# Inverting the sums of exponentials six queries a partition, by way of DRAM, in a routed attention with a squared-ReLU network

## Chip, cores and metric

One core of a Trainium2 chip runs the kernel. The metric is the device time of one execution in microseconds. Before the change the median of three runs is 980.3 us (980.09 to 983.05); the profiled execution spans 978.4 us.

## What is computed

The reference is attention in which a query sees only the keys that have the same nearest centroid, followed by a network with a squared ReLU. There are 4 batches, 8 heads, 768 positions, 64 columns a head and 16 centroids a head.

```python
q_assign = np.argmax(np.einsum('bhsd,hcd->bhsc', q_n, c_n), axis=-1)
k_assign = np.argmax(np.einsum('bhsd,hcd->bhsc', k_n, c_n), axis=-1)
mask = q_assign[:, :, :, None] == k_assign[:, :, None, :]
scores = np.where(mask, scale * q @ k.T, -1e9)
attn = np.exp(scores - np.max(scores, axis=-1, keepdims=True))
attn = attn / (np.sum(attn, axis=-1, keepdims=True) + 1e-09)
x = (attn @ v) laid out as (batch * position, head * column)   # 3072 x 512
h = np.maximum(x @ w_in, 0.0)                                  # 512 -> 2048
out = (h * h) @ w_out                                          # 2048 -> 512
```

The division by the sum is the step that the change is about. The kernel does it after the product with v: it multiplies that product by the inverse of the sum.

## The kernel before

Two heads are worked together as a pair, so there are 16 pairs, four to a batch. A pair's 768 queries are split into two halves of 384 (`h`), and its 768 keys into six chunks of 128, taken two at a time (`c` = 0, 2, 4). One (pair, h, c) is a unit; a pair of the later batches has six units in a row. The list `units` (L711) holds them, and the main loop (L779) walks over it. In each turn it emits, in this order: the scores of unit u, the scaling of halves that were finished earlier (`ends`, L770), the products with v of units that are one or two turns behind, the sums of halves whose v products are complete (`add_up`, L523), rounding of weights, and pieces of other work: the preparation of the next pair (`prep`) and, from L842 and L846, the network of batch 0, which fills TensorE between the attention's products. The networks of batches 1 to 3 follow after the attention (L883), and have their own products (L662, L693).

The order in which instructions stand on each engine is then set by a scheduler that goes by this order of emission, by priorities, and by the buffers that are free. Each engine runs its instructions strictly in the order that results, and nearly all DMA is issued by SyncE's one queue, in order too: a transfer that waits for its data holds up all those behind it.

What the steps around the change do, for pairs 4 to 15 (batches 1 to 3):

- `scores` (L439): TensorE writes the scores of a unit, two key chunks by two heads, into two PSUM tiles `sc` (L447, run by `together`, whose lines are L91 and L94). ScalarE takes the exponential in place (L466). VectorE multiplies by the mask and moves the result to SBUF, one instruction a chunk and head, four a unit (`ex`, L470). The mask compares `qid`, the centroid number of every query, spread over all partitions, with `ids`, those of the keys. There are only two `sc` tiles, so the scores of the next unit wait until `ex` has read this unit's. GpSimd adds up `ex` into `acc` (L480, L482).
- `times_v` (L497): products of `ex` with v, into a PSUM tile `av` for each half. The pool of `av` holds two.
- `add_up` (L523): four products with a column of 2^40 sum `acc` over its partitions, into a PSUM tile `sm` (L532). `sm` has four groups of 32 partitions, one for each head and half of the 384 queries, and each row of a group holds the same 192 sums. VectorE inverts all 128 x 192 of them (`r`, L537). One row of each group goes to DRAM (`far_r`, L540), and comes back spread over 64 partitions a head (`rb`, L543), so that it can multiply `av`, which has columns of v on partitions and queries along the free axis. A copy of the four rows goes to `seen` (L544), for a check at the end that all sums are in range.
- `finish` (L553): VectorE multiplies `av` by `rb` and writes the result to `xT` (L556), which is the network's input. It is emitted one turn after `add_up`, by way of the list `added` (L793, L815).
- The preparation of a pair: q and k are loaded (L109), rewritten by ScalarE (`flat`, L277) and sent to DRAM (`words`, L278), and come back through a DMA that transposes (`qkT`, L288). Products with the centroids (`lg`), a copy (`lgs`, L307), transposes (`lt`) and four VectorE instructions (`mx`, `best` twice, `ids`, L340 to L347) number the clusters; `ids_b` (L359), one transpose, `row` (L401), `far` (L403) and `qid` (L404) spread the numbers of the queries.

Two halves end in each cycle of six units: the second half of a pair (its `sm` comes when the next pair is in its third unit) and the first half of the next (two units later).

Of the kernel before, what the change touches and what calls it, by code (L numbers as in the profile page):

```python
# [8 lines left out]
F32 = mybir.dt.float32  # L9
# [9 lines left out]
P = 128  # L19
# [6 lines left out]
def kernel(  # L26
# [10 lines left out]
    nc = tc.nc  # L37

    B, H, S, D = q.shape
# [6 lines left out]
    HP = H // 2  # L46
    NB = NCH // 2
    TB = NB * P
    NG = B * HP
# [13 lines left out]
    small = ctx.enter_context(tc.tile_pool(name="small", bufs=2))  # L63
# [5 lines left out]
    rbp = ctx.enter_context(tc.tile_pool(name="rbp", bufs=2))  # L69
# [6 lines left out]
    dram = ctx.enter_context(tc.tile_pool(name="dram", bufs=2, space=bass.MemoryType.DRAM))  # L76
# [4 lines left out]
    def bank(name, shape):  # L81
        return ps_f.tile(shape, F32, name=name, tag="f")
# [5 lines left out]
    def together(products, offset=2000):  # L88

        products = iter(products)  # L90
        last = nc.tensor.matmul(**next(products))  # L91
        with tc.high_priority(offset=offset):
            for product in products:
                last = nc.tensor.matmul(**product)  # L94
        return last.ins
# [82 lines left out]
    for _ in range(8):  # L178
# [14 lines left out]
        out=odd[:, 1:2], in0=row_i, scalar1=1.0 / C, scalar2=None, op0=ALU.mult  # L193
    )
    constants = nc.vector.tensor_scalar(
        out=odd[:, 0:1], in0=odd[:, 1:2], scalar1=-1.0, scalar2=1.0, op0=ALU.mult, op1=ALU.add
    ).ins

    seen = const.tile([8 * NG, TB // 2], F32, name="seen")
# [233 lines left out]
    def first_half(pair, h):  # L433
        return pair < HP and h == 0
# [51 lines left out]
    def ones_products(sm, e, rhs, first, last):  # L486

        n, rows = TB // 2, P // 4
        return [
            dict(  # L490
                out=sm[rows * (2 * e + g) : rows * (2 * e + g + 1)], lhsT=ups[:, 0:rows],
                rhs=rhs[:, n * g : n * (g + 1)], start=first, stop=last,
            )
            for g in range(2)
        ]
# [25 lines left out]
    spread_out = {}  # L521

    def add_up(pair, h):  # L523


        b, hp = divmod(pair, HP)
        if first_half(pair, h):
            sm = sums.pop((pair, h))
            nc.scalar.copy(out=xT_of(b, h)[:, hp], in_=av.pop((pair, h)))
        else:  # L530
            total = acc.pop((pair, h))
            sm = bank("sm", [P, TB // 2])  # L532
            one = [ones_products(sm, e, total[:, e], True, True) for e in range(2)]
            together([p for both in zip(*one) for p in both])
        row = 4 * (2 * pair + h)
        r = once.tile([P, TB // 2], F32, name="r")
        nc.vector.reciprocal(out=r, in_=sm)  # L537
        r = r.rearrange("(r p) n -> r p n", r=4)[:, 0]
        far = dram.tile([2, TB], F32, name="far_r")
        nc.sync.dma_start(far.rearrange("e (g n) -> (e g) n", g=2), r)  # L540
        rb = rbp.tile([P, TB], F32, name="rb")
        for e in range(2):
            nc.sync.dma_start(rb[D * e : D * (e + 1)], far[e].partition_broadcast(D))  # L543
        nc.sync.dma_start(seen[row : row + 4], r)  # L544
        spread_out[pair, h] = rb

    def xT_of(b, h):
        if (b, h) not in xT:
            pool = {0: xtp, 1: xt_first, 2 * B - 1: xtp}.get(2 * b + h) or later["xT"]
            xT[b, h] = pool.tile([P, KT, TB], F32, name="xT")  # L550
        return xT[b, h]

    def finish(pair, h):  # L553
        b, hp = divmod(pair, HP)
        x = xT_of(b, h)[:, hp]
        nc.vector.scalar_tensor_tensor(  # L556
            out=x, in0=av.pop((pair, h), x), scalar=UP, in1=spread_out.pop((pair, h)),
            op0=ALU.mult, op1=ALU.mult,
        )
# [5 lines left out]
    def ffn(b, h):  # L565
        gT = []
        for f in range(FT):
            ph = bank("ph", [P, TB])
            for kk in range(KT):
                nc.tensor.matmul(  # L570
                    ph, lhsT=w_in[:, kk, f * P : (f + 1) * P], rhs=xT[b, h][:, kk],
                    start=(kk == 0), stop=(kk == KT - 1),
                )
                if kk < KT - 1:
                    yield TB
            gT.append(gtp.tile([P, TB], F32, name="gT"))
            nc.scalar.activation(out=gT[f], in_=ph, func=ACT.Relu)
            nc.scalar.square(gT[f], gT[f])
            yield TB
        for i in range(NB):  # L580
            po = bank("po", [P, DM])
            for f in range(FT):
                nc.tensor.matmul(  # L583
                    po, lhsT=gT[f][:, i * P : (i + 1) * P], rhs=w_out[:, f],
                    start=(f == 0), stop=(f == FT - 1),
                )
                if f < FT - 1:
                    yield DM
            osb = later["out"].tile([P, DM], F32, name="osb")
            nc.scalar.copy(out=osb, in_=po)  # L590
            nc.sync.dma_start(out_view[b, h * NB + i], osb)
            yield DM
# [148 lines left out]
    def behind_first(u, what=last_logits):  # L741
        return tc.issue_after(what[0]) if u == 0 else ExitStack()
# [23 lines left out]
    added = []  # L766
# [3 lines left out]
    def ends(halves):  # L770
        for pair, h in halves:
            b, hp = divmod(pair, HP)

            with tc.high_priority(offset=1000) if (pair, h) == (HP - 1, 0) else ExitStack():
                finish(pair, h)
            if hp == HP - 1 and (b, h) in PLAIN:
                fill.append(ffn(b, h))

    for u in range(len(units) + 3):  # L779
        if u < len(units):  # L780
            pair, h, c = units[u]
            if (p := next_pair(u)) is not None:
                ahead.extend(prep(p))
            if u in (TWOS, TWOS + 2):

                split_words(HP, int(u > TWOS))
            if c == 0 and u + 3 < len(units) and units[u + 3][0] not in raw_v:
                load_v(units[u + 3][0])

            with behind_first(u):  # L790
                scores(pair, h, c)

        ends(added)  # L793
        added.clear()
        if u < TWOS:
            ready = u - 1
        elif u == TWOS or u % 2 or u >= len(units):
            ready = u

        complete, late = late, []  # L800
        while v_next < min(ready, len(units)):
            pair, h, c = units[v_next]
            times_v(pair, h, c)
            v_next += 1
            if c == NCH - 2:
                (late if h and not HP * NCH <= u < len(units) else complete).append((pair, h))
        for pair, h in complete:
            with tc.high_priority(offset=1000) if first_half(pair, h) else ExitStack():
                add_up(pair, h)
            if h == 1:  # L810
                for d in (qkT, ids, qid):
                    d.pop(pair)
            if h == 1 or pair < HP:
                raw_v.pop(pair)
            added.append((pair, h))  # L815

        rounding += 4
        while rounding >= 3:
            rounding -= 3
            i = next(to_round, None)  # L820
            if i is not None:
                with tc.issue_after(last_exp[0]):
                    round_weights(i)
                if (i := next(loaded, None)) is not None:
                    load_weights(i)
            elif not later:
                early.close()
                for name, bufs in (("xT", 5), ("out", 2)):
                    later[name] = keep.enter_context(
                        tc.tile_pool(name=name + "_late", bufs=bufs, side="right",  # L830
                                     reuse_waits="tile")
                    )
        share = 0
        if u % 2 == 0 or not TWOS < u < len(units):
            n = 2 if TWOS < u < len(units) else 1
            share = max(0, left[0] - RESERVE) * sum(map(density, range(u, u + n)))
            share //= max(1, sum(map(density, range(u, ENDS))))
        goal = left[0] - share

        for i in range(3):  # L840
            if i == 2:
                fill_steps(share * 2 // 3)  # L842
            if ahead:
                with behind_first(u, masked if i else last_logits):
                    (ahead.pop(0) or int)()
        fill_steps(left[0] - goal)  # L846
# [235 lines left out]
```

## Time and profile before

| | us | |
|---|---|---|
| span | 978.4 | |
| TensorE busy | 958.9 | 98% |
| VectorE busy | 562.2 | 57% |
| GpSimd busy | 375.9 | 38% |
| ScalarE busy | 315.4 | 32% |
| r, L537 | 43.4 | 32 x 1357 ns |
| xT, L556, idle before it, waiting for rb | 50.3 | 26 times |

The span has two parts. Up to 538 us attention and the network of batch 0 share the engines; from 538 us to the end the products of L662 and L693 run without a gap, and the chain of work that ended last is these products alone, 44% of the span. In the first part that chain goes through TensorE's products too, and for 13 us before 533 us through r, far_r, rb, xT, ex and acc of the last pair.

In the lists of groups and waits a time is a sum over all instructions of the group, and idle time is given with what ended it. A wait is named after the instruction that waits and the one it waited for. In the timeline the columns are start, duration, engine, line, operation, names, shapes, count, and in brackets the idle time before the first with its releaser; several instructions in a row are merged, and then the duration is that of them all. SPq is the queue of SyncE: there the duration is that of issuing the transfer, and not of the transfer.

### The profile page before, as it was taken

The numbers are of one execution on the slowest core, as the hardware profiler recorded it, in microseconds if no ns is written. First come the engines' busy times: TensorE is split into PE (matmuls) and PEld (weight loads), VectorE is DVE, ScalarE is ACT, GpSimd is POOL, SyncE is SP. The second block draws the span as 40 slices with busy tenths as digits, with TensorE's granted clock in tenths as the row PEclk, the third lists the DMA queues.
The fourth block names the chain that finished last, engine by engine and source line by source line (L and its number), as shares of the span: only waits on it lengthen the run. The fifth ranks groups of instructions, "written<-read, shape, count | busy, mean of one in ns | idle before, by whom it ended". The sixth has DMA issues, their size and how long they took to land.

```text
span 978.4 us, 12070 instructions
## 1 busy us (share of the span) xinstructions
PE 958.9 (98%) x4479; PEld 552.0 (56%) x4479; DVE 562.2 (57%) x913; ACT 315.4 (32%) x511; POOL 375.9 (38%) x277
## 2 busy tenths in 40 slices
PE   7998999999999999999999999999999999999997
PEld 4544444434444444443344556888556888556886
DVE  5767867666566665658654866531556531656331
ACT  5886756344345555544231211000111000111000
POOL 1337757555656556555557331002231002231000
PEclk9999999999999999999999999999999999999999
DMA  9757782444545444443210000000000000000000
GB/s 242 214 180 217 184 200 63 114 116 122 133 115 131 110 119 122 121 115 88 61 37 18 18 1 0 13 26 27 0 1 1 22 22 21 1 1 0 22 22 25
DMA packets 127746, 74.54 MB, mean 76 GB/s; under 512 B 90944, under 2 KB 119104, under 8 KB 127680
## 3 DMA queue, kind: packets, MB, share of 16 engines
q1 hardware_dynamic: 125968, 73.26, 28.3%
q8 instruction: 38, 0.62, 0.3%
q10 hardware_dynamic: 1712, 0.43, 0.2%
q14 instruction: 28, 0.23, 0.1%
HBM read 48.27 MB, written 15.86 MB: 66 GB/s over the span
## 4 chain that ended last, share of the span: by engine, by line
PE 50%; DVE 0%; DMA 0%; POOL 0%; issue 0%; SPq 0%; DVEq 0%; POOLq 0%
PE bank L693 22%; PE bank L662 22%; PE po L583 3%; PE sc L91 1%; PE sc L94 1%; PE av L91 1%; PE av L94 1%; POOL acc L482 0%; DMA rb<-far_r 0%; DVE ex L470 0%; PE sm L91 0%; DMA far_r<-r 0%; DVE r L537 0%; PE lg L91 0%; SPq L543 0%
## 5 line engine op out<-in xcount | busy, mean ns | idle before, releaser
L482 POOL TENSOR_TENSOR acc<-acc,ex 128x768 f32<-128x768 f32 x112 | 205.4, 1834 | 111.0 <-DVE ex L470 97.8
L470 DVE SCALAR_TENSOR_TENSOR ex<-qid,ids,sc 128x384 f32<-128x384 bf16 x288 | 158.0, 609 | 66.6 <-ACT sc L466 48.6
L466 ACT ACTIVATE sc<-sc 128x768 f32<-128x768 f32 x144 | 108.3, 793 | 162.3 <-PE sc L94 144.6
L94 PE MATMUL sc<-qkT 64*128 64x384 f32 x576 | 152.8, 506 | 0.5
L94 PE MATMUL av<-ex,v_raw 128*64 128x384 f32 x576 | 135.6, 491 | 0.0
L651 POOL TENSOR_TENSOR w_s<-w_in 128x256 f32<-128x256 f32 x24 | 18.4, 765 | 276.4 <-PE bank L693 162.0
L632 DVE TENSOR_TENSOR g<-bank,g 128x384 f32<-128x384 f32 x144 | 77.8, 555 | 80.7 <-PE bank L662 79.7
L570 PE MATMUL ph<-xT,w_in 128*128 128x384 f32 x256 | 93.2, 506 | 3.5 <-DVE xT L556 2.8
L693 PE MATMUL bank<-w_out,g 128*128 128x256 f32 x432 | 95.2, 379 | 0.0
L583 PE MATMUL po<-w_out,gT 128*128 128x512 f32 x192 | 92.3, 612 | 0.0
L91 PE MATMUL sc<-qkT 64*128 64x384 f32 x192 | 87.5, 536 | 3.8 <-DVE ex L470 3.8
L693 PEld LDWEIGHTS bank<-w_out,g 128*128 128x128 f32 x432 | 82.1, 190 | 11.8
L632 DVE TENSOR_TENSOR osb<-bank,osb 128x256 f32<-128x256 f32 x54 | 22.1, 423 | 107.6 <-PE bank L693 102.2
L94 PEld LDWEIGHTS sc<-qkT 64*128 64x128 f32 x576 | 65.4, 187 | 27.3 <-issue 4.8
L91 PE MATMUL av<-ex,v_raw 128*64 128x384 f32 x192 | 80.4, 500 | 0.0
L570 PEld LDWEIGHTS ph<-xT,w_in 128*128 128x128 f32 x256 | 46.5, 192 | 43.3 <-issue 13.3
L662 PE MATMUL bank<-xT,w_in 128*128 128x384 f32 x192 | 69.8, 487 | 0.0
L662 PE MATMUL bank<-x_t,w_s 128*128 128x384 f32 x192 | 69.7, 486 | 0.0
L662 PE MATMUL bank<-xT,w_s 128*128 128x384 f32 x192 | 69.7, 486 | 0.0
L480 POOL TENSOR_TENSOR acc<-ex 128x768 f32<-128x768 f32 x28 | 50.8, 1814 | 49.0 <-DVE ex L470 39.8
L94 PEld LDWEIGHTS av<-ex,v_raw 128*64 128x64 f32 x576 | 49.3, 137 | 34.5 <-issue 34.4
L693 PE MATMUL bank<-w_t,g 128*128 128x256 f32 x288 | 65.1, 379 | 0.0
(127 smaller groups left out, 1218.5 us busy)
## 6 DMA issues: line engine op xcount, KB each, us to landing
words<-flat SPq DMA_DIRECT2D x24, 384.0 KB
w_raw<-in_moe_w_in_dram SPq DMA_DIRECT2D x16, 512.0 KB
w_raw<-in_moe_w_out_dram SPq DMA_DIRECT2D x16, 512.0 KB
v_raw<-in_v_dram SPq DMA_DIRECT2D x20, 384.0 KB
rb<-far_r SPq DMA_DIRECT2D x64, 96.0 KB
q_raw<-in_q_dram SPq DMA_DIRECT2D x31, 192.0 KB
k_raw<-in_k_dram SPq DMA_DIRECT2D x31, 192.0 KB
out_dram<-osb SPq DMA_DIRECT2D x23, 256.0 KB
```

Source lines behind the costliest of these rows:

```text
L91: last = nc.tensor.matmul(**next(products))
L94: last = nc.tensor.matmul(**product)
L466: last_exp[0] = nc.scalar.activation(out=t[:, 2 * i : 2 * i + 2] if pair < HP else src, in_=src, func=ACT.Exp, scale=SCALE).ins
L470: nc.vector.scalar_tensor_tensor(out=t[:, 2 * i + e], in0=qid[pair][1][:, h, e], scalar=ids[pair][:, ch % NB, 2 + ch // NB, e : e + 1], in ...
L480: nc.gpsimd.tensor_tensor(out=acc[pair, h], in0=t[:, 0:2], in1=t[:, 2:4], op=ALU.add)
L482: nc.gpsimd.tensor_tensor(out=acc[pair, h], in0=acc[pair, h], in1=t[:, 2 * i : 2 * i + 2], op=ALU.add)
L570: nc.tensor.matmul(ph, lhsT=w_in[:, kk, f * P : (f + 1) * P], rhs=xT[b, h][:, kk], start=(kk == 0), stop=(kk == KT - 1),)
L583: nc.tensor.matmul(po, lhsT=gT[f][:, i * P : (i + 1) * P], rhs=w_out[:, f], start=(f == 0), stop=(f == FT - 1),)
L632: nc.vector.tensor_tensor(out=out, in0=bank, in1=to, op=ALU.add)
L651: nc.gpsimd.tensor_tensor(out=s1, in0=a[1][0], in1=a[1][1], op=ALU.add)
L662: nc.tensor.matmul(bank, lhsT=operands[j][0][:, kk], rhs=operands[j][1][:, kk], start=(kk == 0), stop=(kk == H2 - 1),)
L693: nc.tensor.matmul(bank, lhsT=operands[j][0][:, f], rhs=operands[j][1][:, f], start=(f == 0), stop=(f == F2 - 1),)
```

## The change

In pairs 4 to 14 (`HP <= pair < NG - 1`) the sums are no longer inverted where they are. ScalarE copies the 128 x 192 tile from PSUM (`r`), one row of each group goes to DRAM as sums (`far_s`), and comes back laid out with 64 partitions a head and six queries on each (`few`, 128 x 6). VectorE inverts these six columns. They go to DRAM again (`far_r`), and from there `rb` and `seen` are read as before. The reciprocal thus works on 6 elements a partition instead of 192, and the path from `sm` to `rb` has two round trips through DRAM instead of one. To give it time, the scaling of these halves is emitted two turns behind instead of one. Pairs 0 to 3 and pair 15 keep the old way.

```diff
         row = 4 * (2 * pair + h)
         r = once.tile([P, TB // 2], F32, name="r")
+        if HP <= pair < NG - 1:
+
+            nc.scalar.copy(out=r, in_=sm)
+            far_s = dram.tile([2, TB], F32, name="far_s")
+            nc.sync.dma_start(
+                far_s.rearrange("e (g n) -> (e g) n", g=2),
+                r.rearrange("(r p) n -> r p n", r=4)[:, 0],
+            )
+            few = small.tile([P, 2 * TB // P], F32, name="few")
+            nc.sync.dma_start(few, far_s.rearrange("e (p j) -> (e p) j", p=P // 2))
+            nc.vector.reciprocal(out=few, in_=few)
+            far = dram.tile([2, TB], F32, name="far_r")
+            nc.sync.dma_start(far.rearrange("e (p j) -> (e p) j", p=P // 2), few)
+            rb = rbp.tile([P, TB], F32, name="rb")
+            for e in range(2):
+                nc.sync.dma_start(rb[D * e : D * (e + 1)], far[e].partition_broadcast(D))
+            nc.sync.dma_start(seen[row : row + 4], far.rearrange("e (g n) -> (e g) n", g=2))
+            spread_out[pair, h] = rb
+            return
         nc.vector.reciprocal(out=r, in_=sm)
...
-        ends(added)
-        added.clear()
+        ends([e for due, e in added if due <= u])
+        added[:] = [(due, e) for due, e in added if due > u]
...
-            added.append((pair, h))
+            added.append((u + (2 if HP <= pair < NG - 1 else 1), (pair, h)))
```

## The prediction

> **What bounds the kernel now.** I read the page's busy times first, then the waits of TensorE and VectorE in the stretch that the change touches, then the timeline around single waits. From the page and from the waits of TensorE alone between 200 and 540 us:
>
> ```profile
> PE 958.9 (98%) x4479; PEld 552.0 (56%) x4479; DVE 562.2 (57%) x913; ACT 315.4 (32%) x511; POOL 375.9 (38%) x277
> ```
>
> ```profile
> PE sc L91 <- DVE ex L470: 3.5, 3, 2.5
> PE sm L91 <- POOL acc L482: 0.4, 1, 0.4
> ```
>
> TensorE sets the end: in 340 us it waits 3.9 us. VectorE waits much more in the same stretch (waits of VectorE, 200 to 540 us), but hides it:
>
> ```profile
> DVE xT L556 <- DMA rb<-far_r: 35.8, 20, 3.3
> DVE ex L470 <- DMA qid<-far: 8.7, 2, 4.5
> ```
>
> So removing VectorE work or waits pays only where TensorE waits for VectorE. It does so three times, always a score product (L91) waiting for ex (L470), which must leave the two score banks first: 0.55 us at 225.89, 0.43 at 407.90, 2.48 at 466.27. The timeline of TensorE at the last, and the stretches (us, busy of PE, PEld, DVE, ACT, POOL, clock, DMA) around it:
>
> ```profile
> 466.27 0.61 PE L91 MATMUL sc<-qkT 64*128 64x384 f32 x1 [2.48 <-DVE ex L470]
> ```
>
> ```profile
> 463.23:466.64 3.41, 0.93 (x6) 0.33 (x4) 3.41 (x5) 0.00 (x0) 1.02 (x1) 1.00 1.20 223
> 466.64:470.05 3.41, 3.41 (x10) 1.17 (x7) 1.84 (x5) 1.59 (x2) 2.66 (x2) 0.50 0.13 27
> ```
>
> After the idle window one window runs at clock 0.50 and loses half of 3.41, 1.7 us more. The first two waits follow qid, which the queue issued behind the transpose (waits of VectorE of 4.13 and 4.54 us for it). All that can be won is about 0.8 + 0.6 + 2.5 + 1.7 = 5.6 us.
>
> How tight ex is elsewhere shows in an ordinary pair, timeline of VectorE:
>
> ```profile
> 231.12 1.36 DVE L537 RECIPROCAL r<-sm 128x192 f32<-128x192 f32 x1 [1.14 <-PE sm L94]
> 232.89 2.19 DVE L470 SCALAR_TENSOR_TENSOR ex<-qid,ids,sc 128x384 f32<-128x384 bf16 x4 [0.41 <-ACT sc L466]
> 236.52 0.56 DVE L340 TENSOR_REDUCE mx<-lt 128x24 f32<-128x384 f32 x1 [1.44 <-PE lt L317]
> 237.80 0.56 DVE L556 SCALAR_TENSOR_TENSOR xT<-av,rb 128x384 f32<-128x384 f32 x1 [0.72 <-DMA rb<-far_r]
> ...
> 240.13 2.19 DVE L470 SCALAR_TENSOR_TENSOR ex<-qid,ids,sc 128x384 f32<-128x384 bf16 x4
> ```
>
> Its queue:
>
> ```profile
> 230.23 0.39 SPq L278 DMA_DIRECT2D words<-flat  x1
> 232.50 0.55 SPq L540 DMA_DIRECT2D far_r<-r  x1
> ...
> 234.16 1.12 SPq L543 DMA_DIRECT2D rb<-far_r  x2
> ```
>
> The ex of 240.13 ends at 242.32; TensorE's next scores take the second bank at 242.38. The slack is nil, although TensorE shows no wait.
>
> [...]far_r usually takes 1.6 to 1.65 us to land, 1.96 where it was issued at 353.75 and words had landed only at 355.16.[...]
>
> **The change, part by part.** It touches pairs 4 to 14, 22 halves, two in each cycle of about 30.5 us. TensorE's and GpSimd's instructions stay in the same order; the built orders of the others differ as told here.
>
> Removed from VectorE: 22 reciprocals of 1.36 us, 29.9 us. Added: 22 of six elements; nearest row ids_b (12 elements), 0.18 us, so 4 us. The saving lies on an engine that is 57% busy: worth nothing by itself.
>
> Added to ScalarE: 22 copies of 128x192.[...] The copy stands where the engine waits anyway (from 230.2 to 231.99): nothing.
>
> Added to the queue: a second round trip. Before it was write, read; now it is write sums, read, invert, write, read. Behind its waits in the in-order queue stand q_raw, k_raw, words, qid and the transpose. q_raw goes some 4 us later, but is copied some 20 us after that: nothing.
>
> Moved: xT. In the cycle above, VectorE's new order is: four ex, few, mx to ids_b, two ex, xT, two ex. Two of the ex that TensorE needs by 242.38 now stand behind xT, so behind the whole chain. From the start of sm at 230.52:
> - copy starts at +0.60[...]; sums written at +1.0. words was issued at 230.23 and landed 3.46 us later by the trace, at +3.17;[...] few is issued at +3.4. (Alone it would be +2.6.)
> - few, 128 pieces of 24 B: no such row. Nearest are the centroids (128 x 256 B, 1.83 us) and far (12 x 256 B, median 2.07)[...]. I take 1.85, bounds 1.6 and 2.2: +5.25. Reciprocal done at +5.5 (four ex are done at +4.6).
> - far_r back, 128 pieces of 24 B: 1.63 (four long pieces) to 2.1; I take 1.8: +7.35.
> - rb: issue to xT was 234.16 to 237.80, 3.64, elsewhere 3.37; I take 3.4: +10.75. xT gives way after 0.48, the last two ex take 1.14: done at +12.4.
>
> TensorE needs it at +11.86 (242.38): a wait of some 0.55 us, bounds 0 and 1.3. Of 11 such cycles the built order has two ex behind xT in seven; in four (322 to 412 us) all four stand ahead, and nothing waits. Of the seven, those at 199, 231, 261 and 443 us have this shape: 4 x 0.6. That of 291 has 0.2 us more room: 0.35. At 477 and 509 no words copy is ahead: the chain ends at +11.7, against +11.86 and +11.54: 0 and 0.15. The last also holds back the old reciprocal of pair 15 (519.90), which leads the chain that ended last, by 0.25 more. Sum 3.15 us.
>
> The second half of each cycle: its xT stands before the first ex of the next pair, which waits for qid anyway and has some 2 us of room: nothing, except twice. At 216 us the new order puts qid before the transpose: 0.8 us won. At 399 us it puts qid behind transpose, two rb and seen: before, qid was issued at 402.65; now transpose to 402.55, rb 1.2, seen 0.55: 404.35, 1.7 us later, and ex and TensorE with it: 1.8 lost.
>
> At 466 us: VectorE loses the 1.36 of r and one xT (0.56) ahead of the late ex, but a wait of few and the delayed pair of ex take most of it: ex comes 0.5 us earlier, TensorE's need 0.6 later: 1.1 won. The idle time left, 1.4 of 3.41, should not halve the clock: 1.7 won. The subtraction that made it late (2.56 us against 0.96 for its neighbour) overlaps GpSimd[...]; that stays.
>
> Sum: 3.15 + 1.8 - 0.8 - 1.1 - 1.7 = +1.35; 980.3 + 1.4 = 981.7.
>
> **Rivals.**
> 1. The chain is longer, so xT is a new wait of TensorE: few 2.2 and far_r 2.1 add 0.65 in five cycles and 0.5 in two, 4.3; the wait of 2.2 us at 408 falls in one clock window, 1.7; the window at 466 stays halved, 1.7. 981.7 + 7.7 = 989.4. For it: nil slack, seven copies of it. Against: no row of a transfer with nothing ahead above 2.1.
> 2. The chain fits: sums do not queue behind words (0.6 shorter) and no ex waits for it; 408 loses only what it did before. Then 980.3 - 0.8 - 1.1 - 1.7 = 976.7. For it: far_r is hardly ever late behind words. Against: it is issued 2.2 us after it, the sums only 1.2, and the order of qid at 399 is fixed.
> 3. v banks (two) held longer stop the v products. xT moves from 237.8 to 241.3; the next half starts at 248.92. Against it 7 us of room; if it did cost 1 us a half, 1002.
>
> **How the numbers follow.** My forecast (within 0.3%, 977.4 to 983.2) 0.43; rival 1 and cases between it and the forecast 0.37; rival 3 0.03; rival 2 and cases near it 0.17. Slower is 0.40, faster 0.17. The range ends just below rival 2 (976) and just past rival 1 (990): less than 1 in 10 beyond each end.
>
> **What would show it.** TensorE's waits list sc L91 <- DVE ex with some 7 entries near 211, 243, 273, 304 and 455 of about half a us, and one near 410 of 2. VectorE waits for rb in front of xT with two ex still to come[...]. few <- far_s and far_r <- few take 1.6 to 2.2. No clock of 0.50 at 470. Wrong if few's transfers cost over 2.2, if sums land before words, or if TensorE waits elsewhere.

## Result, and the profile after

The changed kernel takes 986.3 us (983.67 to 990.46), the kernel before 980.2 us beside it on the same chip (977.78 to 983.05; six runs each). The ratio is 1.0064, with a 95% interval of 1.0036 to 1.0091: slower by 0.6%, some 6 us. The profiled execution spans 983.7 us against 978.4. The range (976 to 990) holds the time. The forecast of 981.7 is 4.6 us too low, and the case that was thought likeliest, "within 0.3%" (0.43), did not come; "slower" (0.40) did.

In the changed kernel the lines from `r` (old form) on are 19 higher: `xT` is L575, old `r` L556, the subtractions of the networks L623. New are the copy L539, `far_s` L541, `few` L546 and L547, `far_r` L549, `rb` L552 and `seen` L553.

The busy times of the page, and the waits of TensorE and VectorE between 200 and 540 us (total us, times, longest):

```profile
PE 959.7 (98%) x4479; PEld 551.8 (56%) x4479; DVE 551.1 (56%) x913; ACT 322.5 (33%) x533; POOL 375.9 (38%) x277
```

```profile
PE sc L91 <- DVE ex L470: 5.2, 2, 2.7
PE sc L94 <- DVE ex L470: 1.1, 2, 0.7
```

```profile
DVE xT L575 <- DMA rb<-far_r: 20.1, 10, 5.4
```

TensorE still waits little, and but for 0.4 us for the same thing, ex. Of the three waits of before, the first (226 us) is gone, the second (408) has grown from 0.43 to 2.48, the third (466) is 2.70 instead of 2.48. VectorE's busy time fell by 11.1 us only, where 26 were removed. Its waits in front of xT fell too, from 35.8 us in 20 to 20.1 in 10.

The largest change is at 408. The queue before and after it, from the timelines of SyncE in the kernel before and in the changed kernel (the duration is that of issuing):

```profile
398.03 0.34 SPq L403 DMA_DIRECT2D far<-row  x1
399.03 3.52 SPq L288 DMA_TRANSPOSE qkT<-words  x1
402.65 0.53 SPq L404 DMA_DIRECT2D qid<-far  x1
```

```profile
398.06 0.32 SPq L403 DMA_DIRECT2D far<-row  x1
398.48 0.33 SPq L549 DMA_DIRECT2D far_r<-few  x1
399.06 4.17 SPq L288 DMA_TRANSPOSE qkT<-words  x1
403.29 1.22 SPq L552 DMA_DIRECT2D rb<-far_r  x2
404.55 0.48 SPq L553 DMA_DIRECT2D seen<-far_r  x1
405.14 0.35 SPq L404 DMA_DIRECT2D qid<-far  x1
```

`qid` is issued 2.49 us later. Its data was there long before: far, issued at 398.03 and 398.06, had landed at 399.95 and 399.33, and in both kernels qid went out behind all that stood ahead of it in the queue. So the scores that need its ex wait (timeline of TensorE, changed kernel); two stretches of one clock window each follow (columns as in the prediction):

```profile
409.99 0.98 PE L91 MATMUL sc<-qkT 64*128 64x384 f32 x1 [2.48 <-DVE ex L470]
```

```profile
406.40:409.81 3.41, 1.10 (x4) 0.35 (x2) 1.67 (x4) 0.86 (x2) 0.00 (x0) 1.00 0.27 103
409.81:413.22 3.41, 3.23 (x10) 1.51 (x12) 1.73 (x5) 1.06 (x2) 1.80 (x1) 0.50 0.00 0
```

Of the window from 406.40 TensorE is busy for 1.10 us, and the next runs at clock 0.50. Before, this place had no such window (2.98 of 3.41 busy at the least). At 466 us both kernels have one; in the changed kernel it runs from 471.25 to 474.66, after a window with 1.22 of 3.41 busy.

What each place costs is read by setting the start of every matmul in one profile against the start of the same matmul in the other. At 205 us the two are level (0.07 apart), at 540 us the changed kernel is 5.2 us behind, nearly all of the 5.3 by which the spans differ. Of this, 226 us gives -1.0; 408 us, +3.1; 466 us, +0.6; the ordinary cycles, +0.3 each at 211, 273, 458 and 493 and +0.6 at 242; the last cycle (525), +1.0; small steps back at the start of the cycles take 0.3 off. The sum is +5.1.

Idle time alone tells less than this. In most ordinary cycles the list of waits shows nothing. But these matmuls run overlapped, a pair starting 0.32 us after the last while each takes 0.48, and overlap that is lost is not idle time. At 211 us the last four score products start late and are drawn out (timelines of TensorE, kernel before and changed kernel):

```profile
210.89 1.13 PE L94 MATMUL sc<-qkT 64*128 64x384 f32 x5
211.95 2.84 PE L583 MATMUL po<-w_out,gT 128*128 128x512 f32 x6
```

```profile
210.96 1.41 PE L94 MATMUL sc<-qkT 64*128 64x384 f32 x5
212.30 2.84 PE L602 MATMUL po<-w_out,gT 128*128 128x512 f32 x6
```

The product behind them starts 0.35 us later in the changed kernel, where those ahead start 0.07 later. The expectations below put such a cycle at 0.07 us; the starts say 0.2 to 0.3. For the same reason the wait of 0.43 at 408 in the kernel before costs some 0.9, as the kernel without it shows (e4_before_both, below), so that the 2.48 of wait and the halved window of now, 4.1 together by the kernel without them (e1_qid_first, below), cost some 3.1 more than what stood there before.

### The profile page after: what moved, and what is told of

Same layout as the page of the kernel before. It is cut to its first block, busy times and chain, and to the rows that moved or that the text cites. A ratio compares the mean times of both kernels' runs of the same rounds, so it can differ in the third digit from the quotient of the medians.

```text
span 983.7 us, 12187 instructions
## 1 busy us (share of the span) xinstructions
PE 959.7 (98%) x4479; PEld 551.8 (56%) x4479; DVE 551.1 (56%) x913; ACT 322.5 (33%) x533; POOL 375.9 (38%) x277
## 4 chain that ended last, share of the span: by engine, by line
PE 86%; DVE 4%; DMA 4%; issue 3%; ACT 1%; POOL 1%; SPq 1%; ACTq 0%; DVEq 0%; POOLq 0%
PE bank L712 22%; PE bank L681 22%; PE ph L589 8%; PE po L602 8%; PE sc L91 7%; PE sc L94 6%; PE av L91 5%; PE av L94 5%; DMA rb<-far_r 1%; DVE ex L470 1%; PE sm L91 1%; PE lg L91 1%; POOL w_in L166 1%; DMA k_raw<-in_k_dram 1%; DMA v_raw<-in_v_dram 1%
## 5 line engine op out<-in xcount | busy, mean ns | idle before, releaser
L91 PE MATMUL sc<-qkT 64*128 64x384 f32 x192 | 87.9, 538 | 6.6 <-DVE ex L470 6.6
L91 PE MATMUL av<-ex,v_raw 128*64 128x384 f32 x192 | 80.5, 501 | 0.0
L712 PE MATMUL bank<-w_t,g_s 128*128 128x256 f32 x288 | 65.1, 379 | 0.0
```

The source lines that it names most:

```text
L712: nc.tensor.matmul(bank, lhsT=operands[j][0][:, f], rhs=operands[j][1][:, f], start=(f == 0), stop=(f == F2 - 1),)
```

## Experiments

Theory A is the prediction's, with sizes corrected from the profile: what costs time is qid behind the second round trip (408), a late ex at 466 that the change was wrongly thought to repair, and what little room xT has. Each time is the median of all runs of that kernel (6 to 22); the ratio is to the kernel before on the same chip. The experiments were taken on three chips, on which the kernel before took 980.2, 981.9 and 980.6 us, so kernels of different sections are compared by their ratios.

### The transpose after qid, in the changed kernel

The transpose of the next pair is issued only after the last qid (`e1_qid_first`).

```diff
+        with tc.issue_after(last_qid[0]) if last_qid[0] else ExitStack():
             nc.sync.dma_start(qkT[pair]..., transpose=True)
...
-        nc.sync.dma_start(
+        last_qid[0] = nc.sync.dma_start(
             dst.rearrange("p g e n -> p (g e n)"), ...
-        )
+        ).ins
```

> The changed kernel with one edge more: the transpose of the next pair (qkT) is issued only after this pair's qid. Theory A (the loss is one wait of TensorE near 410 us, 2.5 us, because qid goes out behind the transpose, two rb and seen, and the half clock of 3.4 us after it): that wait and the clock of 0.50 after it vanish, about 4 us off the changed kernel, near 982, ratio to before 1.001 to 1.003. Theory B (the second round trip through DRAM makes xT a wait in many cycles, a little in each): nothing much changes, ratio near 1.006.

Measured 981.3 us, ratio 1.0009 (0.9994 to 1.0023). The largest wait of TensorE from 200 to 540 us, the only one for L91 and ex:

```profile
PE sc L91 <- DVE ex L472: 2.7, 1, 2.7
```

The wait at 408 is gone with its halved window; the 2.7 left is that of 466. By the ratios the edge is worth 0.55%, some 5 us, uncertain by 3; by the profile 2.5 + 1.7 = 4.2, and start against start 4.1. Most of the loss was the place of one DMA in the queue; but some 0.9 of these 4.1 us is the wait that the kernel before had there too.

### The subtractions of x behind the attention, in the changed kernel

The four subtractions (L623) that made ex late at 466 us are held until the last ex of the attention (`e2_late_subs`).

```diff
-        with tc.issue_after(last_exp[0]):
+        with tc.issue_after(last_mask[0]):
             sub(t1, x[0][1], x[0][0])
```

> The changed kernel with the four subtractions of x of batch 1 (L623) held back until the last ex. Both kernels lose some 2.5 us of TensorE and 1.7 us of half clock near 466 us, which the change was forecast to mend and did not. Theory A: that wait has nothing to do with the sums, only with the subtractions ahead of ex on VectorE; held back, it vanishes, 4 us off the changed kernel, near 982, ratio 1.002. Theory B: the wait is made by few and xT ahead of ex, and stays; ratio 1.006.

Measured 982.6 us, ratio 1.0030 (1.0022 to 1.0039). From 200 to 540 us TensorE's waits for L91 are now

```profile
PE sc L91 <- DVE ex L471: 2.8, 1, 2.8
PE sm L91 <- POOL acc L483: 1.6, 1, 1.6
```

of which the 2.8 is at 410 us. The one at 466 has gone with its halved window (2.7 + 1.7; start against start, 4.8), and a smaller new one has come, sm for acc of 1.6 instead of 0.4: the subtractions now overlap the last acc of GpSimd.

### Both edits, in the changed kernel and in the one before

> The changed kernel with both edges (qid before the transpose, subtractions held back). Theory A: both waits gone, 8 us off, near 978, ratio 0.997 to 0.999; what is left are waits of TensorE for ex of under half a us in the cycles in which two ex stand behind xT. Theory B: ratio 1.004 or more.

> The kernel before with the same two edges. Its three waits (225.9, 407.9, 466.3 us) and the half clock vanish: 5 us off, near 975, ratio 0.994 to 0.996. Theory A says that the change then has nothing left to win and costs its small waits: e3_both is 1 to 3 us slower than this. If the change helps by itself, e3_both is the faster one.

The changed kernel with both takes 978.4 us, ratio 0.9981 (0.9971 to 0.9992); the kernel before with both 976.1 us, ratio 0.9958 (0.9945 to 0.9972). Waits of TensorE from 200 to 540 us, first of the changed kernel with both, then of the kernel before with both:

```profile
PE sm L91 <- POOL acc L485: 1.6, 1, 1.6
PE sc L94 <- DVE ex L473: 1.3, 1, 1.3
```

```profile
PE sm L91 <- POOL acc L485: 1.6, 1, 1.6
```

No window between 10 and 970 us of the changed kernel is at half clock. So with both obstacles out of the way the change still costs 2.4 us here, known to some 1 us, and the profiles show where (2.6 us between 205 and 540 us, start against start): 1.6 in the last cycle, with its wait of 1.3, and 0.2 to 0.3 in each of five others. The obstacles were in the kernel before as well, and clearing them there makes it 0.4% faster without the change.

### One half of the change alone

> The old reciprocals of 128x192, with the v products of batch 1 on scaled two units behind instead of one: half of the change alone. The built order of the engines is that of the kernel before but for one ex, and the order of the queue is the same. Theory A (the loss comes from where the second round trip puts qid and from its waits): no change, 980.2 within 0.3%. Rival B (scaling later holds the banks or the order, and so costs the time): near the changed kernel, 986.

> The round trip through DRAM to six queries a partition, with the v products scaled one unit behind as before: the other half alone. The queue's order is that of the changed kernel, qid at 399 us behind the transpose too. Theory A: the whole loss, 986 (984 to 988), with the waits of TensorE at 408 of about 2.5 and at 464 of about 2.7. Rival B: near the kernel before, 980.

The delayed scaling with the old reciprocals: 981.7 us against 981.9, ratio 1.0005 (0.9993 to 1.0018). The round trip with the old delay:

```diff
-            added.append((u + (2 if HP <= pair < NG - 1 else 1), (pair, h)))
+            added.append((u + 1, (pair, h)))
```

989.7 us, ratio 1.0083 (1.0061 to 1.0104), with waits of 2.9 and 2.7 at 413 and 475 us, the places of 408 and 466. The loss belongs to the round trip alone; rival B, and with it rival 3 of the prediction (v banks held longer), is out. The delay does not cost but may help: without it TensorE has three more short waits for ex than the changed kernel (in all 2.5 us in five, instead of 1.1 in two), but by the ratios the two are not told apart. The two runs also separate something that had not been looked at. Of all groups of VectorE between 200 and 540 us (busy us, mean ns, idle before), the second `best` of the delay alone and of the round trip alone:

```profile
L344 DVE TENSOR_TENSOR best<-best,order 128x384 bf16<-128x384 bf16 x10 | 6.6, 663 | 0.3
```

```profile
L344 DVE TENSOR_TENSOR best<-best,order 128x384 bf16<-128x384 bf16 x10 | 16.2, 1619 | 0.3
```

The same ten instructions take 9.6 us more. Why is told below.

### Pair 14 left as before

The last cycle's wait was there in every profile of the changed form so far. Here pair 14 keeps the old reciprocals.

```diff
-        if HP <= pair < NG - 1:
+        if HP <= pair < NG - 2:
```

> The changed kernel with both edges of e3_both, and with pair 14 (the last that the change touches) left with the old reciprocals and the old delay. If the late chain of pair 14[...] is what is left of the change's cost: the wait of 1.3 us at 515 us is gone and the time is 1.3 us below e3_both's, 977.1. If the small waits of 0.07 us and other terms carry it: within 0.5 us of 978.4.

Measured 979.7 us, ratio 0.9980 (0.9969 to 0.9991): no gain against the ratio of 0.9981 of e3_both. In its profile the wait at 515 is gone, but another of 1.3 us stands at 244 us. Timeline of TensorE, and of VectorE before it:

```profile
244.49 0.92 PE L94 MATMUL sc<-qkT 64*128 64x384 f32 x4 [1.30 <-DVE ex L473]
```

```profile
237.69 0.19 DVE L550 RECIPROCAL few<-few 128x6 f32<-128x6 f32 x1 [2.23 <-DMA few<-far_s]
...
242.73 0.56 DVE L578 SCALAR_TENSOR_TENSOR xT<-av,rb 128x384 f32<-128x384 f32 x1 [1.19 <-DMA rb<-far_r]
243.21 2.18 DVE L473 SCALAR_TENSOR_TENSOR ex<-qid,ids,sc 128x384 f32<-128x384 bf16 x4
```

`few` was issued at 234.32 and its reciprocal could run at 237.69, 3.4 us later instead of 1.6 to 1.8. Now xT does wait for rb with two ex behind it, as the prediction had it for five of the cycles.

### The subtractions where there is room

The kernel before with the edge of qid; the subtractions stand behind earlier ex, first three of them and then all four.

```diff
+        with tc.issue_after(masks[-21]):
             sub(t1, x[0][1], x[0][0])
             sub(t2, x[1][1], t1)
             sub(t4, t2, x[1][0])
+        with tc.issue_after(masks[-13]):     # masks[-1] in e8_spread_subs
             sub(x[0][1], x[1][1], x[0][1])
```

> The kernel before with the edge of qid, and the subtractions of batch 1's x spread: three behind the ex that ends about 497.6 us in the profile of e4_before_both, where VectorE then has 3.8 us free and GpSimd 4.2, and one behind the last ex. There they should not stretch the last acc of GpSimd. The one wait left in that profile, sm for acc of 1.6 us, shrinks to the 0.4 of the kernel before: 976.1 - 1.2 = 974.9. If a subtraction delays the ex of 501.4 instead, the gain is lost: 976 to 977.

> The kernel before with the edge of qid and all four subtractions of batch 1's x where VectorE and GpSimd have room: three behind the ex that ended about 498 us in the profile of e8_spread_subs, the fourth behind the one that ended about 509. No subtraction then overlaps the last acc; the wait of sm for acc, 1.6 us in e4_before_both and 1.0 in e8_spread_subs, is 0.4: about 0.6 us under e8_spread_subs, ratio to before about 0.995. If the wait stays at 1.0, something other than the subtractions stretches that acc.

976.5 us, ratio 0.9958 (0.9939 to 0.9977), and 976.9 us, ratio 0.9960 (0.9943 to 0.9977). The wait of sm for acc fell from 1.6 to 1.0, where 0.4 was expected, and in the second run to 0.4; the time does not show it, and a gain of 0.6 to 1.2 us is within these intervals.

### The same edits in the changed kernel

> The changed kernel with the same two edits as e9_best_before; the two differ by the change alone, with no half clock and no wait for qid left in either. Theory A (the round trip has no room in front of xT, and a transfer of the chain that is held up reaches TensorE): the profile has waits of 0.07 us in some five cycles and one of about 1.3, at the last cycle; the time is 1.5 to 2.5 us above e9_best_before. Rival (what was left in e3_both came from the subtractions near the last acc, not from the chain): equal to e9_best_before within 0.5 us.

976.0 us, ratio 0.9958 (0.9942 to 0.9974), against 976.9 and 0.9960 of e9_best_before: no difference, but one of up to some 2 us could not be told by these runs. The only wait of TensorE that its list from 200 to 540 us shows is sm for acc, 0.4.

The expected wait of 1.3 at the last cycle is missing. Theory A was applied wrongly there, since the edit had also changed VectorE's order in that cycle. Timeline of VectorE, first in e3_both and then in e10_best_after:

```profile
512.05 1.14 DVE L473 SCALAR_TENSOR_TENSOR ex<-qid,ids,sc 128x384 f32<-128x384 bf16 x2 [4.04 <-POOL acc L485]
514.94 0.56 DVE L578 SCALAR_TENSOR_TENSOR xT<-av,rb 128x384 f32<-128x384 f32 x1 [1.75 <-DMA rb<-far_r]
515.41 1.13 DVE L473 SCALAR_TENSOR_TENSOR ex<-qid,ids,sc 128x384 f32<-128x384 bf16 x2
```

```profile
516.73 2.19 DVE L473 SCALAR_TENSOR_TENSOR ex<-qid,ids,sc 128x384 f32<-128x384 bf16 x4 [2.82 <-ACT sc L469]
...
519.81 0.56 DVE L578 SCALAR_TENSOR_TENSOR xT<-av,rb 128x384 f32<-128x384 f32 x1 [0.90 <-DMA rb<-far_r]
```

rb is late in both (far_r was issued 2.64 us before it in e10_best_after, 3.18 in e3_both; far_r usually lands after 1.4), but in the second no ex of that group stands behind xT. The late transfer then costs no wait. The 0.2 to 0.3 us of the ordinary cycles are still there, and start against start the profile of e10_best_after loses 1.1 us to that of e9_best_before between 205 and 540 us. So the change still costs TensorE about 1 us here, less than the runs can tell.

The same with pair 14 left as before:

> e10_best_after with pair 14, the last that the change touches, left with the old reciprocals and the old delay. If its late far_r makes most of what the change still costs: 1.3 us below e10_best_after, and no wait of TensorE near 515. If the late transfers fall anywhere in the chain, a wait of that size turns up in another cycle and the time is within 0.5 us of e10_best_after.

976.7 us, ratio 0.9957 (0.9944 to 0.9971): no difference, as the wait that it was to remove was already gone.

### A queue of its own for the sums

In e10_best_after, `far_s` issued by ScalarE.

```diff
-            nc.sync.dma_start(
+            nc.scalar.dma_start(
                 far_s.rearrange("e (g n) -> (e g) n", g=2),
```

> e10_best_after with the write of the sums issued by ScalarE, so on a queue of its own that has no words transfer ahead. If the sums land late only because words is ahead of them in the ring (the step of the prediction): their landing falls from 2.3 to 2.7 us to 1.6 in every cycle, the small waits of 0.07 us go, and the time is 0.3 to 0.5 us below e10_best_after, with the tail's wait still there. If the landing stays above 2.2, it is not the order of the ring but the engines' load that makes it late.

980.8 us, ratio 1.0006 (0.9985 to 1.0026), slower than e10_best_after. By the trace the sums land 2.5 us (median, 200 to 540 us) after their issue, against 2.2 in e10_best_after; where no words transfer is under way it is 1.6 in both. At 232 us the four pieces of 768 bytes moved only from 233.67 to 233.82, on a queue of their own (the page has 176 packets more in q10 than that of the changed kernel, and 176 fewer in q1), while the 768 pieces of the words transfer were moved from 232.53 to 234.11. The sums landed at 234.34, and words at 234.46. In the other cycles with a words transfer the sums land 0.2 us before words to 1.2 us after it, but for one in which words took 2 us longer than usual. So it is not their place in the queue that makes the sums late: with a words transfer under way they are late from another queue too. By what means, these runs do not show.

TensorE waits 2.2 us for ex from 200 to 540 us in all, one of the waits for a qid that the new order put behind rb and seen; the rest of the slower time is not taken apart.

## Why the prediction was right or wrong

**Right.** What bounds the kernel, and where it could lose: each wait of TensorE after the change, but for the old 0.4 for acc, is one for ex, and the one that grew is the one named, qid behind transpose, rb and seen. The wait at 226 us went (-1.0, -0.8 forecast). The copy takes 0.32 us, and no wait for it is seen; few's reciprocal 0.19 (0.18); in the cycles that the prediction works out the sums land behind words 2.2 to 2.7 us after their issue (2.3). Holding the v banks cost nothing that could be measured.

**408 us: the size failed.** The step "1.8 lost" is 3.1. The transpose took 4.17 us to issue where 3.52 was taken, so the wait grew by 2.05; and a halved window came, whose 1.7 was put into rival 1 only. A wait of some 2.2 us, which the step itself gave, is nearly as long as the one at 466 that had just been read as halving the next window. Whether it would halve one could not be known: by the runs it depends on how the wait lies to windows that the kernel does not set (last section), and of eight such waits six did.

**466 us: the step failed.** "1.1 won" and "1.7 won" were 0, and 0.6 more was lost. The 1.7 stood for a window with 1.4 us idle and full clock behind it. The kernel before has such a one, from 12.67 us (TensorE busy for 1.99 of 3.41 us, the next window at clock 1.00), but in the one that came, from 467.84, TensorE was busy for 1.22 only, and the next ran at 0.50. The step took the work removed ahead of the late ex as time won. But the subtractions did not start when VectorE got there; the timelines of VectorE show it, first in the kernel before and then in the changed one:

```profile
456.17 0.96 DVE L604 TENSOR_TENSOR x_t<-xT 128x768 f32<-128x768 f32 x1 [0.61 <-ACT sc L466]
...
462.97 2.10 DVE L604 TENSOR_TENSOR x_t<-x_t,xT 128x768 f32<-128x768 f32 x1
464.99 2.18 DVE L470 SCALAR_TENSOR_TENSOR ex<-qid,ids,sc 128x384 f32<-128x384 bf16 x4
```

```profile
459.30 1.40 DVE L623 TENSOR_TENSOR x_t<-xT 128x768 f32<-128x768 f32 x1 [1.37 <-ACT sc L466]
...
463.65 2.56 DVE L623 TENSOR_TENSOR xT<-xT 128x768 f32<-128x768 f32 x1
466.14 2.56 DVE L623 TENSOR_TENSOR x_t<-x_t,xT 128x768 f32<-128x768 f32 x1
468.62 2.18 DVE L470 SCALAR_TENSOR_TENSOR ex<-qid,ids,sc 128x384 f32<-128x384 bf16 x4
```

The first waits for ScalarE's exponential, to which the program ties it (`issue_after(last_exp[0])`); the last two run beside GpSimd's acc and take 2.56 each, where before they took 2.56 and 2.10. What VectorE saved, 1.35 and 0.55 less 0.18 of few, became idle time ahead of these four (0.76) and stretch in them (0.44 in the first, 0.46 in the last). e2_late_subs shows that these four instructions were the cause of the wait.

**Seven cycles with two ex behind xT: about the right size for five, wrong mechanism.** The forecast had xT wait for the chain of DMA, 0.35 to 0.6 us in five cycles. By the trace few takes 1.6 to 1.8 us and far_r 1.4 to 1.8 (1.85 and 1.8 were taken), and rb, from the first of its two issues to its landing, 3.2 to 3.6 (3.4 was taken, up to xT). So rb has landed 0.2 to 0.7 us before VectorE reaches xT: in the cycle of 211 us at 209.04, with xT at 209.71. What makes the last ex late there is VectorE's own work. Its timeline in the kernel before and in the changed kernel:

```profile
207.09 0.73 DVE L344 TENSOR_TENSOR best<-best,order 128x384 bf16<-128x384 bf16 x1
...
208.53 2.19 DVE L470 SCALAR_TENSOR_TENSOR ex<-qid,ids,sc 128x384 f32<-128x384 bf16 x4
```

```profile
206.27 1.68 DVE L344 TENSOR_TENSOR best<-best,order 128x384 bf16<-128x384 bf16 x1
...
209.71 0.55 DVE L575 SCALAR_TENSOR_TENSOR xT<-av,rb 128x384 f32<-128x384 f32 x1
210.18 1.13 DVE L470 SCALAR_TENSOR_TENSOR ex<-qid,ids,sc 128x384 f32<-128x384 bf16 x2
```

The last ex ends at 211.31 instead of 210.72. Some 0.5 of this is xT, which now stands ahead of it and needs its own time though it waits for nothing; 0.1 is L344. Without xT ahead of it L344 starts at 206.27 instead of 207.09, but ends at 207.95 instead of 207.82: it ends 0.41 us after GpSimd's acc, which ends at 207.54. In all fourteen profiles it takes 0.56 us where it does not meet acc, and its overlap with acc plus 0.42, within 0.01, wherever they overlap by over 0.2 us. So about 9.5 of the 26 us that the change frees on VectorE come back as a longer L344. The prediction saw that the slow subtraction overlaps GpSimd, and did not ask which other instruction would move under acc. What the longer L344 alone costs TensorE is not shown, since no run moved it.

**The last cycle: right place, size off.** 0.15 + 0.25 were forecast, 1.0 were lost start against start, and 1.6 in e3_both (with waits of 0.7 and 1.3), since far_r took some 3 us there. That is the one cycle in most profiles where xT really waits for rb with ex behind it: in the changed kernel the exponentials for these ex end at 521.81, xT starts at 523.86, after 1.51 us of waiting for rb, and the ex behind it only at 524.33; e10_best_after shows that the order decides whether it costs.

**Order in the queue: right number, wrong reason.** That the sums land no earlier than words, because they stand behind it in the same queue, was the author's estimate. The sums did land as late as forecast, with words: of the 19 in the changed kernel, from 170 to 545 us, that were issued with a words transfer under way, 18 landed between 0.14 us before words and 0.21 after it, and the one of 416.69, where words took 5.35 us, 1.45 before it. But e11_own_ring has them no earlier on another queue, so the common queue is not what makes them late.

In sum, +1.35 was forecast and 5.1 came. At 466 the forecast is 3.4 too low (-2.8 for +0.6) and at 408 1.3 too low (1.8 for 3.1); 226 us and the cycles take 0.9 off (-0.8 and 3.15 for -1.0 and 2.4). That the range holds the time, and that the cycles come near their 3.15, is in part luck: two of the three terms of rival 1 came, the halved windows at 408 and 466, and its slow few and far_r did not.

The kernel before with the edge of qid and the subtractions moved (e4_before_both, e8_spread_subs, e9_best_before), and the changed one with the same as in e9_best_before (e10_best_after, e12_best_short), all stand at ratios of 0.9957 to 0.9960, 0.4% faster than the kernel before and by the ratios 1.0% faster than the changed one; between them there is nothing to choose.

## What to carry to other kernels

Ask of each added transfer which urgent one it is put ahead of in its queue: here qid waited in it for over 5 us after its data had landed (399.33 to 405.14), and one edge in the order of the queue was worth 4 to 5 us; the 26 us of VectorE work that the change removes were worth nothing that could be measured. An engine that is freed ahead of a late instruction helps only if nothing else sets that instruction's start: look for its gate, and for the GpSimd instruction that it will now run beside (L344: 0.56 us without acc, up to 1.69 beside it). A wait of over 2 us on TensorE should be priced with a halved window behind it, worth up to 1.7 us, as a chance and not as certain (six of eight waits of 2.4 us or more here). And the idle gap can be less than what a wait costs (0.43 at 408 us in the kernel before cost some 0.9): set the starts of the same matmuls against each other.

## What was not expected of the hardware

A transfer of 3 KB sometimes takes 1 to 2 us longer: in the changed kernel far_r lands 1.42 us after its issue (median), but 3.06 us after the issue at 517.54. The page of the profile lists a queue of instructions:

```profile
q8 instruction: 38, 0.62, 0.3%
```

that is, pieces of 16 KB. In the traces of the kernel before and of the changed one, one comes about every 27 us (14 between 165 and 545 us) and takes 0.9 to 1.5 us. In the changed kernel one runs from 518.60 to 519.55, and eight of the 128 pieces of that far_r are moved at 519.53 to 519.59, the others by 518.55. In e3_both one runs from 509.01 to 510.14, and the last eight of the 128 pieces of far_r, as many as fall to one of 16 DMA engines if all get the same, are moved at 510.12 to 510.18, 2.1 us after its issue; in e7_both_short one starts at 235.4, and eight of few's pieces are moved at 236.55 instead of 235.62 like the others. On this reading every further round trip in a chain is one more chance to meet such a piece. This is read from the times in the traces, which do not name the engine of a piece; no run moved those pieces.

The clock was halved after a window in which TensorE had been busy for 1.10 or 1.22 of 3.41 us, not idle throughout. So a window that was two thirds idle was enough here.

The windows do not follow the kernel. Within a trace the changes of the clock lie whole multiples of 3.413 us apart (409.81 and 471.25 in the changed kernel, 18 times; 91.17 and 466.64 in the kernel before, 110 times), so it matters how a wait falls across two of them. Of the eight waits of 2.4 us or more between 165 and 540 us in all profiles, six fell nearly whole into one window (0.6 to 1.3 us busy), and the next was halved. The other two did not: in e6_few_only the wait of 2.7 us at 475, and in e5_defer_only one of 2.49 us that ends at 468.29, spread over two windows of which the emptier was busy for 1.83 and 1.87 us. The stretches of e5_defer_only:

```profile
463.47:466.89 3.42, 2.34 (x16) 0.78 (x12) 3.42 (x3) 0.56 (x1) 2.73 (x2) 1.00 0.80 196
466.89:470.30 3.41, 1.87 (x9) 0.77 (x10) 2.43 (x6) 0.80 (x1) 0.96 (x1) 1.00 0.66 149
470.30:473.71 3.41, 3.41 (x8) 1.33 (x8) 2.07 (x4) 1.38 (x2) 3.33 (x3) 1.00 0.21 77
```

The same wait in the kernel before was followed by a halved window, and start against start it cost 1.3 us more. Where the limit lies is not shown: a window with 1.82 us busy, at 162.33 in e9_best_before, was followed by a halved one, and one with 1.78, at 123.10 in the changed kernel, was not.
